# A gated mix of attention and feed-forward: the order of the first key and query products, of the last projection products, an eviction split in two, and the last stores

## The chip, the cores and the metric

The kernel runs on one NeuronCore of a Trainium2 chip. Its engines, as the profile names them, are PE (TensorE, matrix products, with PEld for its weight loads), DVE (VectorE), ACT (ScalarE), POOL (GpSimd) and SP (SyncE, which here issues most of the DMAs). The metric is device time in microseconds (us), lower is better. All times in this text are us unless marked otherwise; a time such as 12.80 is a place in the profiled execution, counted from the start of its span.

## The reference, cut to what matters

```python
x = A_x                                            # 1 x 2048 x 512, bf16
g = sigmoid((x * gate_w).sum(-1, keepdims=True))
q, k, v = split(x @ wqkv)                          # 32 heads of 16
p = softmax((q @ k.T) * 16 ** -0.5)
a = merge_heads(p @ v) @ wo
b = (silu(x @ w_gate) * (x @ w_up)) @ w_down       # 512 -> 1792 -> 512
return g * a + (1 - g) * b
```

## The kernel before, in words

The queries are cut into four blocks of 512 (`QB`), the heads into eight groups of four (`G`), which makes 32 units (`UNITS`) of 16 key tiles (`KT`). For each unit and key tile PE makes scores `s_t` in PSUM, two heads at a time in one tile of 128 x 1024; ACT turns each into `e_t` with one exponential; PE then multiplies it with the values into `o_ps`, the output product. A part of the tiles goes another way: PE makes `d_t`, and DVE computes the exponential of it in several steps over `y_t`, `z_t` and `u_t`, with an addition done by a DMA from POOL's queue. The first column of each head's values is one, so `o_ps` also holds the softmax denominators. When a unit is done, `post` (L900) evicts `o_ps` to `osb`.

Around this a planner in the kernel (`Plan`, `Pacer`) orders the other work, which is the projections of queries, keys and values and the feed-forward. It keeps estimated times of PE, DVE and ACT and writes each engine's instructions in one fixed order; `mm`, `act`, `vec` and `queue` record that order, so most instructions have the lines L158, L161 and L170 of these helpers. Each engine works through its own list in order. The planner starts its clocks after the opening, so the opening and the end are written out by hand.

**The opening (L178 to L1062).** The input is needed transposed, as `xT`: four blocks of 128 features (`dc` 0 to 3). For the first 1024 tokens, blocks 0 and 1 come by transposing DMAs, which SP issues one after the other; the rows of blocks 2 and 3 come by a plain DMA into `x_rows` (a part of `wd_t`) and are turned on PE by products with the identity (`turn`, L1022). Block 3's turned form is evicted by ACT into `xT`, block 2's by DVE in two halves. The weights of the first four heads come by ACT's queue and are spread by ACT into `wpad[1]` (keys) and `wpad[0]` (queries), with gaps between the heads; this is the padding copy of L241 to L244. `keep_warm` (L999) makes products whose result nobody reads. Then come the key products into `kp0` (two per block), the query products into `qp0` (one per block) and, after each block but the last, one `keep_warm`. Behind them:

- DVE takes the largest key of each row (`largest`, `kpart`) and makes a bound from it (`k_neg`, `kneg1`),
- ACT takes the size of the queries (`aq0`) and evicts the keys into `kaug`,
- PE makes the first values (`v0`, tile `vp`) and adds the bound to the queries (`bound_add`),
- DVE makes two variants of the queries from the sum (`q0a`); the first scores need them.

**The end (from L1451).** The last query block's output is `o @ wo`, scaled by the gate, for four tiles of 128 tokens (`tq` 0 to 3). All but the last unit's part is summed ahead: tiles 0 and 1 in `a_l_a` and `a_l_b`, tiles 2 and 3 in the two halves of one PSUM tile `al`, which takes a buffer of the scores. Each sum has five products (`last_rows`): three with normalised heads (`on`), one with the unit before the last (`osb`, `wo_l`), one that brings in the feed-forward part (`bblk`, `ident`). `tail(0)` writes the first five of al's ten products ahead of the last output product, `tail(1)` the other five behind it. For the last unit the denominators are gathered by four small products `dt`, inverted by DVE (`rt`), spread by sixteen small products `rps`, multiplied by DVE into `on_l` (four pieces), and four more products finish the sums. DVE scales and evicts tiles 0 and 2, ACT tiles 1 and 3, and each of the four tiles is stored by its own DMA of 128 KB, from SP for DVE's and from ACT's queue for ACT's.

Of the kernel before, what the change touches and what calls it, by code (L numbers as in the profile page):

```python
# [8 lines left out]
ACT = mybir.ActivationFunctionType  # L9
# [3 lines left out]
F32 = mybir.dt.float32  # L13
# [66 lines left out]
def kernel(  # L80
# [12 lines left out]
    nc = tc.nc  # L93
    P = 128
# [6 lines left out]
    NB = H // 8  # L101
    DC = D // P
    FC = F // P
    KT = S // P
    QBW = 512
    QB = S // QBW
    TQ = QBW // P
    assert H * DH == D and D % P == 0 and F % P == 0 and S % QBW == 0 and G == 8 and TQ == 4
    out_f = out.flatten_outer_dims()
    inv_sqrt_dh = 1.0 / math.sqrt(DH)  # L110
    VC = DH + 1
    UNITS = QB * G
# [26 lines left out]
    ps_s = ctx.enter_context(tc.tile_pool(name="ps_s", bufs=2, space=bass.MemoryType.PSUM))  # L139
# [6 lines left out]
    def ordered(ins):  # L146
        i = ins.ins
        if i.engine in last_of:
            tc.add_manual_dep(
                i, last_of[i.engine].name,  # L150
                mybir.DependencyInfo(mybir.DependencyClass.NoSync, mybir.DependencyReason.DATA),
                reason="order",
            )
        last_of[i.engine] = i
        return ins

    def mm(*args, **kw):
        return ordered(nc.tensor.matmul(*args, **kw))  # L158

    def act(*args, **kw):  # L160
        ordered(nc.scalar.activation(*args, **kw))  # L161
# [10 lines left out]
    vec = Ordered(nc.vector)  # L172
    queue = Ordered(nc.sync)
# [11 lines left out]
    for c0 in (D, 0):  # L185

        nc.scalar.dma_start(out=wqk[:, :, c0:c0 + 64],
                            in_=A_wqkv[:, c0:c0 + 64].rearrange("(dc p) c -> p dc c", p=P))
# [6 lines left out]
    for c0 in (D, 0):  # L195
        queue.dma_start(out=wqk[:, :, c0 + 64:c0 + D],
                          in_=A_wqkv[:, c0 + 64:c0 + D].rearrange("(dc p) c -> p dc c", p=P))
# [19 lines left out]
    mt = big.tile([P, FC, QBW], BF16, name="mt")  # L217
# [20 lines left out]
    def ones_rows(engine, g):  # L238

        engine.memset(kaug[:, g, :].bitcast(F32), 1.0019378662109375)  # L240
    for i in (1, 0):  # L241
        act(out=wpad[i][:, :, :].rearrange("p dc (j c) -> p dc j c", c=32)[:, :, :, 1:1 + DH],
            in_=wqk[:, :, i * D:i * D + 64].rearrange("p dc (j c) -> p dc j c", c=DH), func=ACT.Copy)
        ones_rows(nc.vector, 2 - i)  # L244
    ident = const.tile([P, P], BF16, name="ident")
    nc.gpsimd.memset(ident[:], 1.0)
    nc.gpsimd.affine_select(out=ident[:], in_=ident[:], pattern=[[-1, P]], compare_op=ALU.is_equal,
# [13 lines left out]
    for h in range(8):  # L261
        c = 2 * (h % 4) + h // 4
# [29 lines left out]
    owed = []  # L292
# [19 lines left out]
    def spend_v(cost, ready=0.0, key=None):  # L312

        if key is not None and key == plan.last:
            cost += 0.13
        plan.last = key
        plan.dve = max(plan.dve, ready) + cost

    def pay(i=0):
        ready, cost, f, c, key = owed.pop(i)  # L320
        spend_v(cost, ready, key)
        keep, plan.chain = plan.chain, None
        f()
        plan.chain = keep
        if c is not None:
            c.owed -= 1
            if c.done():
                c.done_at = plan.slot

    def m_ready(n=1):  # L330

        t = sorted(b for b in banks if b is not None)
        return t[n - 1] if len(t) >= n else None

    def stuck():
        if d_wait:
            pay_d()
        elif owed:
            pay()
        else:  # L340
            emit_piece(pace.cur)

    def m_tile(name):
        while m_ready() is None:
            stuck()
        i = min((i for i in range(3) if banks[i] is not None), key=lambda i: banks[i])
        plan.pe = max(plan.pe, banks[i])
        banks[i] = None
        held[i] = ps_m[i].tile([P, QBW], F32, tag=f"m{i}", name=name)
        return held[i]  # L350
# [15 lines left out]
    def force(c):  # L366
        for a in c.after + c.begun:
            force(a)
        while not c.out():
            while c.cond is not None and not c.cond():  # L370
                if owed:
                    pay()
                else:
                    for f in at.pop(min(at)):
                        f()
            emit_piece(c)
        while c.owed:
            pay()
# [292 lines left out]
    scaled = set()  # L671
# [180 lines left out]
    o_of = {}  # L852
    closed = 0
    o_end = [0.0]
    done_a = [0] * UNITS
    pvs = [0] * UNITS
# [33 lines left out]
    osbs = {}  # L890
# [9 lines left out]
    def post(un):  # L900
        qb, g = UNIT[un]
        osbs[un] = osb0[qb] if g == 0 else work.tile([P, QBW], BF16, tag="osb", name="osb")
        if un == 0:
            assert part_scaled
            vec.tensor_tensor(out=osbs[un][:, :], in0=o_of.pop(un)[:, :], in1=o_part, op=ALU.add)
        else:
            vec.tensor_copy(out=osbs[un][:, :], in_=o_of.pop(un)[:, :])

# [10 lines left out]
    def recip16(o, i):  # L919
        with nc.allow_low_precision(reason="bf16 reciprocal of softmax denominators is plenty accurate here"):  # L920
            vec.reciprocal(o, i)
# [36 lines left out]
    here_done = []  # L958
    a_ps = []
# [9 lines left out]
            a_ps.extend([pa, pb])  # L969
        return two_banks(NB + 1, "a_l", last_rows(0), last_rows(1), keep, stop=False)  # L970

    def tail(k):

        if k == 0:
            for c in sorted(pace.chains, key=lambda c: c.deadline):
                force(c)
            while owed:
                pay()
            assert here_done and len(scaled) == TQ
            al = ps_s.tile([P, 2 * QBW], F32, tag="s", name="al")  # L980
            a_ps.extend([al[:, 0:QBW], al[:, QBW:2 * QBW]])
        todo = [(tq, i) for tq in (2, 3) for i in range(NB + 1)]
        for tq, i in todo[:5] if k == 0 else todo[5:]:
            w, r = last_rows(tq)(i)
            mm(a_ps[tq][:, 0:D], lhsT=w, rhs=r, start=(i == 0), stop=False)

# [12 lines left out]
    def keep_warm(n):  # L999
        for _ in range(n):  # L1000
            mm(warm[:, :], lhsT=idle[:, 0:P], rhs=idle[:, :], start=True, stop=True)
# [26 lines left out]
    tp = ps_s.tile([P, 2 * QBW], F32, tag="s", name="tp")  # L1028
    turn(DC - 1, [tp[:, 0:QBW], tp[:, QBW:2 * QBW]])
    act(out=xT[:, DC - 1, 0:2 * QBW], in_=tp[:, :], func=ACT.Copy)  # L1030
    tps = [m_tile("tp") for _ in range(2)]
    turn(DC - 2, tps)
    for k in range(2):
        vec.tensor_copy(out=xT[:, DC - 2, k * QBW:(k + 1) * QBW], in_=tps[k][:, :])
        m_free(tps[k], 0.0)
    keep_warm(1)
    arrived = (0, 3, 2, 1)
    for dc in arrived:
        for tb in range(2):
            mm(kp0[:, tb * QBW:(tb + 1) * QBW], lhsT=wpad[1][:, dc, :], rhs=xT[:, dc, tb * QBW:(tb + 1) * QBW],  # L1040
               start=(dc == arrived[0]), stop=(dc == arrived[-1]))
        mm(qp0[:, :], lhsT=wpad[0][:, dc, :], rhs=xT[:, dc, 0:QBW], start=(dc == arrived[0]), stop=(dc == arrived[-1]))
        if dc != arrived[-1]:
            keep_warm(1)
    largest(0, kp0[:, :])
    k_neg(kneg1, 0, idle[:, 0:P])
    act(out=aq0, in_=qp0[:, :], func=ACT.Abs)
# [19 lines left out]
    pace = Pacer()  # L1067
# [60 lines left out]
    for qb in range(1, QB):  # L1128
        d = qb * KT
# [5 lines left out]
    for qb in range(QB):  # L1135
        for b in range(NB):
            d = UNIT.index((qb, max(2 * b, 1))) * KT
# [30 lines left out]
    for qb in range(QB):  # L1168
# [18 lines left out]
        for tq in range(TQ):  # L1187
            c = pace.add(down_pieces(qb, tq), 0 if qb else 100, a0 + per * (0.6 + 0.3 * (tq + 1) / TQ if qb < QB - 1 else 0.68 + 0.32 * (tq + 1) / TQ), (gus if tq == 0 else prev) + fin_prev + gates)
# [202 lines left out]
    while au < UNITS:  # L1391
# [10 lines left out]
        if room > 0.02:  # L1402
# [6 lines left out]
            c = side(room + SLACK)  # L1409
# [23 lines left out]
        n = au * KT + at_  # L1433
# [5 lines left out]
    while closed < UNITS or vops or added or vcur:  # L1439
        fill_dve()  # L1440
        while owed and owed[0][0] <= plan.pe:
            pay()
        if plan.slot < SLOTS + 1:
            begin(plan.slot + 1)
            pace.credit = max(pace.credit, 2.0)
        if vcur:
            emit_d()
            continue
        c = side(2.0)
        if not pv_list(plan.pe) and c is not None:  # L1450
            put_piece(c)  # L1451
            continue
        if closed == UNITS - 1 and pvs[closed] == KT - 1:
            tail(0)
        next_pv()
    for c in sorted(pace.chains, key=lambda c: c.deadline):
        force(c)
# [10 lines left out]
    assert not at  # L1468
    un = UNITS - 1
    osb = osbs[un]  # L1470
    tail(1)
    dt = m_tile("dt")
    for tq in range(TQ):
        mm(dt[:, 4 * tq:4 * tq + 4], lhsT=osb[:, tq * P:(tq + 1) * P], rhs=sel_t[:, :], start=True, stop=True)
    rt = work.tile([P, 4 * TQ], BF16, tag="rt", name="rt")
    recip16(rt[:, :], dt[:, 0:4 * TQ])
    rps = ps_s.tile([P, 2 * QBW], F32, tag="s", name="rps")
    for tq in range(TQ):
        for j in range(4):
            mm(rps[32 * j:32 * j + 32, tq * P:(tq + 1) * P],  # L1480
               lhsT=rt[:, 4 * tq + j:4 * tq + j + 1].broadcast_to([P, 32]), rhs=ident[:, :],
               start=True, stop=True, tile_position=(0, 32 * j), skip_group_check=True)
    on_l = work.tile([P, QBW], BF16, tag="rd", name="on_l")
    for tq in range(TQ):
        cs = slice(tq * P, (tq + 1) * P)
# [4 lines left out]
    for tq in range(TQ):  # L1490
        t = (QB - 1) * TQ + tq
        if tq % 2 == 0:
            vec.tensor_scalar(out=mt[:, tq, :], in0=a_ps[tq][:, 0:D], scalar1=gval[:, t:t + 1], scalar2=None, op0=ALU.mult)
        else:
            act(out=mt[:, tq, :], in_=a_ps[tq][:, 0:D], func=ACT.Identity, scale=gval[:, t:t + 1])
        (queue if tq % 2 == 0 else nc.scalar).dma_start(out=out_f[t * P:(t + 1) * P, :], in_=mt[:, tq, :])

# [28 lines left out]
```

## Time and profile before

| | us |
|---|---|
| median of 4 runs | 830.71 |
| the runs | 830.58, 832.01, 830.29, 830.85 |
| the profiled execution, its time | 832.21 |
| the profiled execution, its span from first to last instruction | 830.5 |
| busy in the span: PE, DVE, ACT, POOL | 787.1, 795.6, 810.9, 102.2 |
| first exponential starts | 14.56 |
| last exponential ends | 821.65 |
| mean granted PE clock | 0.996 |

The profiled execution is 1.50 longer than the median of the runs, and 0.20 longer than the longest of them. Of its time 1.71 lies outside the span. The busy times are sums over the whole span; the views by stretch tell where each engine is full. In a timeline line the columns are start, duration, engine, source line, operation, what is written from what with the shapes, how many, and in brackets the idle time before it and what ended it. A tile's name is followed by `<-` and its inputs, and buffer numbers are left out. Equal instructions that follow each other closely are merged into one line.

### The profile page before, as it was taken

What the parts mean: (1) busy time and instruction counts of PE and PEld (TensorE: products, weight loads), DVE (VectorE), ACT (ScalarE), POOL (GpSimd) and SP (SyncE); (2) the same over time, 40 slices, a digit from 0 to 9 for tenths busy, and PEclk for the clock granted to TensorE, in tenths of its full rate; (3) what the DMA queues carried; (4) which work ended last, traced back from release to release, by engine and by line L of the source; (5) the groups of instructions that cost most, each with busy time, mean ns of one, the idle gap of its engine ahead of it and who ended that gap; (6) DMA issues with size and microseconds to landing.
All of it is one profiled execution on the core that took longest, in us unless ns stands there. A gap on an engine that the chain in (4) does not pass through costs nothing. (4 is left out here: it accounts for less than half of the span.)

```text
span 830.5 us, 20397 instructions
## 1 busy us (share of the span) xinstructions
PE 787.1 (95%) x8118; PEld 233.7 (28%) x8119; DVE 795.6 (96%) x1175; ACT 810.9 (98%) x912; POOL 102.2 (12%) x124
## 2 busy tenths in 40 slices
PE   8999999999999999999999999999998999999996
PEld 3322332322222222222222222222222222222222
DVE  6799999999999999999999999999999999999994
ACT  4999999999999999999999999999999999999996
POOL 5010011010001100101111110101111101111100
PEclk9999999999999999999999999999999999999999
DMA  7034346565544445564444464544435365453323
GB/s 178 2 64 89 71 88 130 120 146 102 111 102 84 81 90 124 107 125 82 82 82 95 84 141 86 122 91 97 80 64 111 78 123 112 102 100 71 77 61 77
DMA packets 100647, 79.54 MB, mean 96 GB/s; under 512 B 75696, under 2 KB 88584, under 8 KB 100552
## 3 DMA queue, kind: packets, MB, share of 16 engines
q0 software_dynamic: 12960, 47.19, 30.7%
q1 hardware_dynamic: 85720, 30.60, 15.9%
q8 instruction: 63, 1.03, 0.5%
q10 hardware_dynamic: 1872, 0.46, 0.3%
q14 instruction: 32, 0.26, 0.1%
HBM read 21.36 MB, written 2.34 MB: 29 GB/s over the span
## 5 line engine op out<-in xcount | busy, mean ns | idle before, releaser
L161 ACT ACTIVATE e_t<-s_t 128x1024 bf16<-128x1024 f32 x844 | 787.8, 1110 | 3.6 <-PE s_t L158 3.4
L158 PE MATMUL s_t<-qx,kaug 64*128 64x512 bf16 x1336 | 274.0, 383 | 24.9 <-ACT e_t L161 21.5
L170 DVE TENSOR_SCALAR y_t<-d_t 128x512 uint16<-128x512 f32 x360 | 234.4, 681 | 1.4 <-PE d_t L158 1.2
L158 PEld LDWEIGHTS <-kaug 64*128 64x128 bf16 x2048 | 111.8, 93 | 340.6 <-issue 331.1
L158 PE MATMUL o_ps<-e_t,vaug 128*32 128x512 bf16 x1688 | 168.1, 390 | 0.3 <-DVE osb L170 0.3
L158 PE MATMUL d_t<-qx,kaug 64*128 64x512 bf16 x296 | 102.0, 380 | 2.3 <-DVE y_t L170 1.5
L792 POOL DMA_DIRECT2D y_t<-u_t x45 | 44.4, 988 | 362.0 <-PE s_t L158 178.5
L158 PEld LDWEIGHTS <-vaug 128*32 128x32 bf16 (+1 forms) x2060 | 50.7, 93 | 122.8 <-issue 121.8
L158 PE MATMUL gu<-xT,wg 128*32 128x512 bf16 x896 | 76.8, 383 | 0.1
L158 PE MATMUL dps<-wd_t,mt 128*32 128x512 bf16 x896 | 76.1, 383 | 0.2
L792 POOL DMA_DIRECT2D y_t<-kaug x39 | 40.5, 1038 | 283.7 <-DVE kaug L170 108.1
L158 PE MATMUL gu<-xT,wu 128*32 128x512 bf16 x896 | 73.4, 382 | 0.1
L170 DVE TENSOR_SCALAR y_t<-y_t 128x2048 uint16<-128x2048 uint16 x90 | 61.5, 684 | 6.5 <-DMA y_t<-u_t 3.8
L170 DVE TENSOR_SCALAR z_t<-y_t 128x2048 uint16<-128x2048 uint16 x90 | 61.8, 687 | 1.0
L170 DVE TENSOR_TENSOR u_t<-u_t 128x2048 f16<-128x2048 f16 x45 | 55.0, 1221 | 0.9
L170 DVE TENSOR_TENSOR u_t<-u_t,z_t 128x2048 f16<-128x2048 f16 x45 | 54.7, 1215 | 0.1
L170 DVE TENSOR_TENSOR kaug<-kaug 128x2048 f16<-128x2048 f16 x39 | 47.7, 1222 | 0.9
L158 PE MATMUL s_t<-q,kaug 64*128 64x512 bf16 x212 | 43.5, 383 | 4.7 <-ACT e_t L161 4.2
L170 DVE TENSOR_TENSOR kaug<-kaug,z_t 128x2048 f16<-128x2048 f16 x39 | 47.4, 1216 | 0.1
L170 DVE SCALAR_TENSOR_TENSOR mt<-gs,gu 128x512 bf16<-128x512 bf16 x56 | 38.2, 683 | 2.4
L161 ACT ACTIVATE th<-gu 128x512 bf16<-128x512 f32 x56 | 38.2, 682 | 0.0
L170 DVE SCALAR_TENSOR_TENSOR gs<-th,gu 128x512 bf16<-128x512 bf16 x56 | 37.9, 677 | 0.1
(134 smaller groups left out, 560.1 us busy)
## 6 DMA issues: line engine op xcount, KB each, us to landing
y_t<-u_t POOLq DMA_DIRECT2D x45, 512.0 KB, 5.0
y_t<-kaug POOLq DMA_DIRECT2D x39, 512.0 KB, 5.1
wg<-in_B_w_gate_dram SPq DMA_DIRECT2D x56, 128.0 KB
wu<-in_B_w_up_dram SPq DMA_DIRECT2D x56, 128.0 KB
y_t<-wd_t POOLq DMA_DIRECT2D x6, 512.0 KB, 5.0
on<-osb SPq DMA_DIRECT2D x120, 16.0 KB
rb<-rr SPq DMA_DIRECT2D x15, 128.0 KB
wd_t<-in_B_w_down_dram SPq DMA_DIRECT2D x7, 256.0 KB
```

What stands on the lines that cost most here:

```text
L158: return ordered(nc.tensor.matmul(*args, **kw))
L161: ordered(nc.scalar.activation(*args, **kw))
L170: return lambda *a, **kw: ordered(f(*a, **kw))
L792: nc.gpsimd.dma_start(out=ya, in_=ua, accum_op=ALU.add)
```

## The change

There are five edits, the first two in the opening and the other three at the end:

1. The padding copy of the query weights (`pad(0)`) stands behind ACT's eviction of the turned block, no longer ahead of it.
2. All eight key products stand ahead of the four query products; the blocks are taken in the order 0, 2, 3, 1 and not 0, 3, 2, 1; the three `keep_warm` products between the blocks are gone.
3. The ten products of `al` are taken by kind and not by tile, and spread in other places: three ahead of the last two output products, three behind them, two behind `dt`, two behind `rps`.
4. The last `osb` is evicted in two halves of 256 columns, one by DVE and one by ACT.
5. The four stores of 128 KB become two of 256 KB, tiles 0 and 1 from SP and tiles 2 and 3 from ACT's queue.

```diff
-    for i in (1, 0):
+    def pad(i):
         act(out=wpad[i][:, :, :].rearrange("p dc (j c) -> p dc j c", c=32)[:, :, :, 1:1 + DH],
             in_=wqk[:, :, i * D:i * D + 64].rearrange("p dc (j c) -> p dc j c", c=DH), func=ACT.Copy)
-        ones_rows(nc.vector, 2 - i)
+
+    pad(1)
+    for g in (1, 2):
+        ones_rows(nc.vector, g)
...
+        elif un == UNITS - 1:
+            o = o_of.pop(un)
+            vec.tensor_copy(out=osbs[un][:, 0:QBW // 2], in_=o[:, 0:QBW // 2])
+            act(out=osbs[un][:, QBW // 2:QBW], in_=o[:, QBW // 2:QBW], func=ACT.Copy)
         else:
             vec.tensor_copy(out=osbs[un][:, :], in_=o_of.pop(un)[:, :])
...
-    def tail(k):
-
-        if k == 0:
-            for c in sorted(pace.chains, key=lambda c: c.deadline):
-                force(c)
-            while owed:
-                pay()
-            assert here_done and len(scaled) == TQ
-            al = ps_s.tile([P, 2 * QBW], F32, tag="s", name="al")
-            a_ps.extend([al[:, 0:QBW], al[:, QBW:2 * QBW]])
-        todo = [(tq, i) for tq in (2, 3) for i in range(NB + 1)]
-        for tq, i in todo[:5] if k == 0 else todo[5:]:
+    rest = [(tq, i) for i in range(NB + 1) for tq in (2, 3)]
+
+    def tail_ready():
+        for c in sorted(pace.chains, key=lambda c: c.deadline):
+            force(c)
+        while owed:
+            pay()
+        assert here_done and len(scaled) == TQ
+        al = ps_s.tile([P, 2 * QBW], F32, tag="s", name="al")
+        a_ps.extend([al[:, 0:QBW], al[:, QBW:2 * QBW]])
+
+    def tail(n):
+
+        for _ in range(n):
+            tq, i = rest.pop(0)
             w, r = last_rows(tq)(i)
             mm(a_ps[tq][:, 0:D], lhsT=w, rhs=r, start=(i == 0), stop=False)
...
     act(out=xT[:, DC - 1, 0:2 * QBW], in_=tp[:, :], func=ACT.Copy)
+    pad(0)
     tps = [m_tile("tp") for _ in range(2)]
...
-    arrived = (0, 3, 2, 1)
+    arrived = (0, 2, 3, 1)
     for dc in arrived:
         for tb in range(2):
             mm(kp0[:, tb * QBW:(tb + 1) * QBW], lhsT=wpad[1][:, dc, :], rhs=xT[:, dc, tb * QBW:(tb + 1) * QBW],
                start=(dc == arrived[0]), stop=(dc == arrived[-1]))
+    for dc in arrived:
         mm(qp0[:, :], lhsT=wpad[0][:, dc, :], rhs=xT[:, dc, 0:QBW], start=(dc == arrived[0]), stop=(dc == arrived[-1]))
-        if dc != arrived[-1]:
-            keep_warm(1)
...
-        if closed == UNITS - 1 and pvs[closed] == KT - 1:
-            tail(0)
+        if closed == UNITS - 1 and pvs[closed] >= KT - 2 and not a_ps[2:]:
+            tail_ready()
+            tail(3)
         next_pv()
...
-    tail(1)
+    tail(3)
     dt = m_tile("dt")
...
     recip16(rt[:, :], dt[:, 0:4 * TQ])
+    tail(2)
     rps = ps_s.tile([P, 2 * QBW], F32, tag="s", name="rps")
...
+    tail(len(rest))
     on_l = work.tile([P, QBW], BF16, tag="rd", name="on_l")
...
-        (queue if tq % 2 == 0 else nc.scalar).dma_start(out=out_f[t * P:(t + 1) * P, :], in_=mt[:, tq, :])
+        if tq % 2:
+            (queue if tq == 1 else nc.scalar).dma_start(
+                out=out_f[(t - 1) * P:(t + 1) * P, :].rearrange("(i p) d -> p i d", p=P), in_=mt[:, tq - 1:tq + 1, :])
```

In the instruction lists that the two kernels build, everything between the opening and the last output products stands in the same order on every engine.

## The prediction

> **What bounds the kernel now.** I read the busy times of stretches first, because the edits touch only the first 15 us and the last 12. Columns: stretch, its length, busy us of PE, PEld, DVE, ACT, POOL, granted PE clock, DMA share, GB/s.
>
> ```profile
> 26.00:800.00 774.00, 742.47 (x7710) 217.94 (x7709) 761.86 (x1107) 772.61 (x869) 89.22 (x88) 1.00 0.48 96
> ```
>
> ACT is busy 772.61 of 774.00 us, with exponentials. So a head start of the exponentials is handed on to the last one, and a saving behind the last one counts in full. Next the timeline of the start (start us, us, engine, line, operation, what ended the idle time):
>
> ```profile
> 7.40 0.44 ACT L161 ACTIVATE mt<-wqk 128x256 bf16<-128x256 bf16 x1 [1.28 <-DMA wqk<-in_A_wqkv_dram]
> 7.73 1.00 ACT L161 ACTIVATE xT<-tp 128x1024 bf16<-128x1024 f32 x1
> ...
> 11.13 1.23 DVE L170 TENSOR_REDUCE kpart<-kp 128x1 f32<-128x1024 f32 x1 [3.11 <-PE kp L158]
> ...
> 12.80 0.40 PE L158 MATMUL qp<-mt 128*32 128x512 bf16 x4 [0.56 <-DVE mt L170]
> 13.33 1.41 DVE L170 TENSOR_SCALAR mt<-qp,vsel 128x512 bf16<-128x512 f32 x2 [0.58 <-PE qp L158]
> ...
> 14.56 1.03 ACT L161 ACTIVATE e_t<-s_t 128x1024 bf16<-128x1024 f32 x1 [0.57 <-PE s_t L158]
> ```
>
> The first exponential stands at the end of one chain: key products, their maximum, the bound, the query variants, the scores. The eviction of the turned block sat behind a padding copy that waited for a DMA until 7.40. The clock comes from windows of 3.41 us:
>
> ```profile
> 5.30:8.71 3.41, 2.86 (x24) 1.49 (x23) 1.29 (x2) 1.76 (x3) 3.02 (x13) 1.00 1.32 224
> ...
> 12.13:15.54 3.41, 1.65 (x20) 0.61 (x20) 2.63 (x6) 2.58 (x4) 0.00 (x0) 1.00 1.02 287
> 15.54:18.95 3.41, 3.41 (x28) 0.69 (x20) 3.18 (x7) 1.99 (x3) 0.00 (x0) 0.50 0.46 158
> ```
>
> In the window from 12.13 PE was busy 48%, and in the next its clock is 0.50: five key pieces (20 products) take 15.12 to 17.0, where five at the usual 0.216 would need 1.1. The chain of waits gives the end:
>
> ```profile
> 820.91 0.34 PE o_ps L158 x4
> 821.25 0.32 PE al L158
> 821.57 0.05 issue
> 821.62 0.81 PE al L158 x3
> 822.44 0.33 PE o_ps L158 x4
> 822.77 1.19 PE al L158 x5
> 823.95 0.09 PE dt L158 x4
> 824.04 0.02 issue
> 824.07 0.27 DVE rt L170
> 824.34 0.04 issue
> 824.38 0.44 PE rps L158 x16
> ```
>
> The last exponential ended at 821.65, but its output product waited for five projection products, to 822.37; then five more kept dt from an osb that was ready at 823.51.
>
> **What the skill says.** "TensorE: Matmul & The Clock Gate", Part 1: PE's clock halves after an idle window of about 3.4 us, and the windows run free of the kernel. The trace agrees in size (15.54 to 18.95 is 3.41), and shows that 48% busy is idle enough while 84% (first window) is not. "PSUM — Partial Sum Buffer", PSUM bank collisions: ACT and DVE may not read one bank's quadrant at once, even in different columns; they have to be ordered. The trace agrees for one tile: ACT's read of al at 827.07 waited 0.56 for DVE's. "DMA: Bandwidth & Descriptors", Anatomy of one DMA: most of a DMA's fixed time lies behind its last byte. Here the last store's packets end near 829.15 and the span at 830.5.
>
> **Start.** Removed: three warming products (0.216 each). Moved: four query products behind eight key products, the second padding copy behind the turned block's eviction, and block 2 ahead of block 3. No DMA moves.
> 1. Turned block: its products end near 6.4, so ACT evicts from about 6.5 to 7.5, off the path; the padding copy then runs to about 7.95, and the query products need it only after 9.
> 2. Key products: the first still waits for its transposed block until 7.69. Six products at 0.216 end at 8.98. The seventh needs the other transposed block, of which before shows only that it was there by 10.50. In the DMA view SP's queue had moved 2064 packets by 6.2 and 3204 by 8.0; the rows of x and each transposed block take 1040. So the first block's packets ended near 6.4 (seen at 7.69) and the second's, at 3120, near 7.9; with a like delay it lands near 9.15. So the last key product starts at 9.37, not 10.72: the maximum starts at about 9.80 instead of 11.13, **1.33 earlier**. Bounds: 1.5 with no wait, 0 if the block lands near 10.4.
> 3. Bound: maximum 1.23 and k_neg 0.35 allow it at 11.45. PE first does four query products (0.86) and vp (1.10) from 9.58, to 11.5. So 11.5, not 12.80.
> 4. Query variants, scores and exponential keep their distances (12.80 to 14.56 is 1.76): first exponential 13.28, **1.28 earlier**. ACT's key eviction moves from 12.39 to 11.25 behind Abs and ends at 12.37, before the scores at 12.86. DVE's and PE's later work hangs on the same products and moves along. The later loads are in time: the last block of xT has its packets by 12.6, so lands near 13.8, and the fourth of the key pieces needs it near 14.5; the rest of the weights, by 17.3, has later users.
>
> The clock is a second effect. With pieces at 0.216 the third exponential of before would start at 16.7, not 17.67, and the fourth at 17.6, not 19.15: the slow window cost this execution about **1.5**. It took 832.21 us; the runs' median is 830.71, with 830.29, 830.58, 830.85 and one at 832.01. The gap of 1.50 is what the slow window costs, so I take it that most timed runs don't have it: it needs a window that holds the idle stretch. After the change PE idles about 1.2 us in that stretch (11.9 to 12.86, 13.25 to 13.52) instead of 1.8, so a window is at least 64% busy, which should spare the clock. Against the median this gives nothing.
>
> **End.**
> 1. Two of the five projection products go behind the last output product. PE: three al from 820.85, two output products from 821.61 and 821.83 (the exponential ends at 821.65). The last ends near 822.23 instead of 822.77: **-0.54**.
> 2. osb is split: 256 columns on DVE, 256 on ACT. By the instructions of the changed program as built, ACT waits for DVE's half, not for PE. DVE: 448 columns took 0.619 and 512 0.682, so 256 about 0.42. ACT copies: 512 took 0.59, 1024 0.996, so 256 about 0.39. In series, with the 0.03 seen at al: 0.84 instead of 0.69, **+0.15**; osb is whole at 823.12. ACT's waits on old DMAs are long over. Bounds: -0.3 if the halves overlapped, +0.3 with a slower hand-over.
> 3. dt's second half needs ACT's half: recip at 823.47 instead of 824.07. Of the other seven al products three lie under the eviction, two under recip, two under on_l. The last two hold the first on_l product to about 824.82 (825.18 before), so DVE's a_l_a eviction starts at 825.26, not 825.64, and the last ACT eviction at 826.69, not 827.07: **-0.38** is left.
> 4. Two stores of 256 KB for four of 128. The last now starts 0.38 earlier but carries twice the bytes. Before, its packets took 0.52 us for 128 KB, at up to 358 GB/s; another 128 KB is **+0.36**. Issue: 0.36 before; other DMAs with 512 and 1024 rows took 0.46 to 0.74, so 0 to +0.3 more. On SP the first store now waits for ACT's half too (825.96), with no store behind it; its packets are gone before the last one's.
> Sum of the end: about 0, from -0.3 to +0.5.
>
> **Forecast:** -1.28 and about 0: -1.3 on 830.71, **829.4 us**. A measurement of this kernel can tell about 0.2%, 1.66 us, from no change, so this counts as no difference, though it should be a real gain.
>
> **Rivals.**
> A, the forecast, 60%: 828.7 to 830.0 of its own (start 1.1 to 1.5, end -0.3 to +0.4, median's noise); about a third of it lies beyond 1.66, most of that because before's own runs hold a slow window now and then.
> B, the slow window is in all of before's runs and gone after, and the profile's 1.5 us are its overhead: -1.3 -1.5 = **827.9**. For it: the window stands plainly in the trace. Against: three of four runs lie 1.4 below the other. 22%.
> C, the transposed block lands near 10.4: the key products wait, and the query products are pushed behind them: gain at most 0.2, **830.5**. Only the bound of 10.50 speaks for it; the packet count against. 13%.
> D, slower: without the warming products and with PE waiting for blocks, a window from about 7 to 10.4 counts as idle, and query products, vp, bound, scores and key pieces run at half clock: +0.9, +0.7, +0.2, +0.2 and +1.1 is 3.1, less 1.3: **832.5**. It decides if the limit lies above the 80% that PE would be busy there; 84% held the clock. 5%, of which 3 are slower by over 1.66.
>
> **Chances.** Faster: 20 from A and 22 from B, 0.42. Slower: 0.03. Same: the rest of A, C and D, 0.55. Range: 827.7 to 830.3 holds A, most of B and part of C.
>
> **What would show it.** First exponential near 13.3, maximum near 9.8, seventh key product waiting for a DMA until about 9.15; no 0.50 stretch after 15. At the end, last output product 0.2 after the last exponential's end instead of 0.7; ACT's osb half starting just as DVE's ends; a last store whose packets take about 0.9. I'd be wrong in the start if the key products waited past 9.6, in the end if the last store's packets took as long as before.

## The result, and the profile after

| | before | after |
|---|---|---|
| median of the runs | 831.02 (53 runs, 830.16 to 833.08) | 829.52 (34 runs, 828.29 to 832.59) |
| the profiled execution, its time | 832.21 | 829.32 |
| its span | 830.5 | 827.6 |
| first exponential starts | 14.56 | 13.33 |
| last exponential ends | 821.65 | 818.85 |

The ratio is 0.998, with a 95% interval of 0.9975 to 0.9985: a gain of 1.50 us, just inside the 0.2% that were called no difference. One run of e1 (1581.61) and one of the runs of before beside e1 to e4 (3272.12) lie far outside all the others and are left out of every interval and count below.

The busy times of the middle stretch, in the columns of before:

```profile
26.00:797.00 771.00, 739.63 (x7687) 216.97 (x7683) 758.99 (x1101) 769.90 (x866) 89.19 (x88) 1.00 0.48 96
```

ACT is busy 769.90 of 771.00, so it still bounds the kernel; how much of a head start it hands on is read further down. The timeline of the opening of after:

```profile
6.97 1.02 ACT L161 ACTIVATE xT<-tp 128x1024 bf16<-128x1024 f32 x1 [0.82 <-PE tp L158]
...
7.89 0.43 ACT L161 ACTIVATE mt<-wqk 128x256 bf16<-128x256 bf16 x1
7.94 1.89 PE L158 MATMUL kp<-xT,mt 128*128 128x512 bf16 x8 [0.35 <-DMA xT<-in_A_x_dram]
...
9.87 1.22 DVE L170 TENSOR_REDUCE kpart<-kp 128x1 f32<-128x1024 f32 x1 [1.38 <-PE kp L158]
...
11.56 0.40 PE L158 MATMUL qp<-mt 128*32 128x512 bf16 x4
...
13.33 1.94 ACT L161 ACTIVATE e_t<-s_t 128x1024 bf16<-128x1024 f32 x2 [0.51 <-PE s_t L158]
...
15.51 2.86 ACT L161 ACTIVATE e_t<-s_t 128x1024 bf16<-128x1024 f32 x3 [0.24 <-PE s_t L158]
```

The eight key products are one line of 1.89, so nothing stops them once they have begun; the maximum follows at 9.87, the bound at 11.56 with no idle bracket in front of it, the first exponential at 13.33 and the third at 15.51. The same stretches of 3.41 us as before show that the clock stays up:

```profile
12.12:15.53 3.41, 2.36 (x30) 0.94 (x34) 3.08 (x5) 2.66 (x5) 0.00 (x0) 1.00 1.03 282
15.53:18.94 3.41, 3.41 (x44) 0.85 (x36) 3.34 (x8) 3.41 (x4) 0.00 (x0) 1.00 0.48 167
```

The granted clock (third column from the end) is 1.00 in both, where before had 0.50 in the second. ACT is full there (3.41) where it had 1.99. The chain of waits at the end of after:

```profile
818.87 0.57 PE o_ps L158 x8
819.45 0.02 issue
819.47 0.44 DVE osb L170
819.91 0.02 issue
819.93 0.39 ACT osb L161
820.32 0.05 issue
820.37 0.20 PE dt L158 x2
820.57 0.45 PE al L158 x2
821.02 0.36 PE rps L158 x16
821.39 0.02 issue
821.41 0.88 DVE on_l L170 x4
822.29 0.66 DVE mt L170
822.96 0.67 DVEq L1538
823.63 0.02 issue
823.65 0.69 ACT mt L161
```

The last output product no longer stands behind five projection products; the two halves of `osb` stand one behind the other; and the last eviction, ACT's, stands behind DVE's (822.96 to 823.65).

**Where the time came from, in the profiled pair.** I followed the start of the n-th exponential in both traces. Before is later by 1.23 at the first, by 2.72 at the fourth, by 2.79 at the last (820.47 against 817.68). From the last exponential's end the span goes on for 8.75 after and 8.85 before, 0.10 less. So 832.21 - 829.32 = 2.89 is 1.23 (the chain of the opening) + 1.49 (the slow clock window, which before's profiled run had) + 0.07 (the middle) + 0.10 (the end).

A caution goes with this sum. The builds e3, e4, e7, e10 and e12 below have their first exponential within 0.06 of after's, and up to the 140th each keeps its distance from after to 0.02; but their last one starts between 0.89 earlier (e10) and 1.45 later (e4). So one pair of traces shows only to about a microsecond how much of a head start reaches the end.

**In the medians.** Of before's 53 runs, 18 are above 831.5; the median of the other 35 is 830.72. After has one run in 34 above 831.5; but its runs lie lower, so the same limit catches fewer of them: three (830.58, 830.66 and 832.59) lie 1.0 or more above its median. So 1.20 of the 1.50 is there against the lower runs of before too, and 0.30 comes from the share of the higher ones; what the 1.20 is made of the medians don't say (see e5). Over all the sets of runs of before below, 59 of 149 are above 831.5, the medians of the two parts lying 1.5 to 1.6 apart in each set, which is close to the 1.49 that the slow window cost in the profiled run.

### The profile page after: what moved, and what is told of

It reads as the page before. It is cut to its first block, busy times and chain, and to the rows that moved or that the text cites. A ratio compares the mean times of both kernels' runs of the same rounds, so it can differ in the third digit from the quotient of the medians.

```text
span 827.6 us, 20391 instructions
## 1 busy us (share of the span) xinstructions
PE 785.2 (95%) x8115; PEld 233.0 (28%) x8116; DVE 795.0 (96%) x1175; ACT 811.2 (98%) x913; POOL 102.2 (12%) x124
```

## The experiments

Theory: the gain is the head start of the opening's chain, about 1.25, and the end gives nothing. Rivals: the gain is the slow clock window alone; the end gains and loses something that cancels. "Stretch" is the time from the start of the last exponential to the end of the span, which the traces give to a hundredth (830.51 before, 827.61 after): 10.04 before, 9.93 after. The medians of before beside the runs were 830.91 (e1 to e4), 831.41 (e5 to e8) and 831.40 (e9 to e12).

**e1 and e8: the edits of the opening alone.** The kernel before, with

```diff
-    for i in (1, 0):
+    def pad(i):
...
+    pad(0)
...
-    arrived = (0, 3, 2, 1)
+    arrived = (0, 2, 3, 1)
...
+    for dc in arrived:
...
-        if dc != arrived[-1]:
-            keep_warm(1)
```

> The kernel before with the two edits of the opening alone (padding copy behind the eviction; key products ahead of query products, no warming products between). If the gain comes from the opening and is handed on to the last exponential: first exponential near 13.3 (14.56 before), the stretch from the last exponential's end to the span's end unchanged at 8.85, median 1.2 to 1.7 below before. If the gain comes from the end: first exponential earlier, but the last one ends where it did, median within 0.3 of before.

Measured: 829.92 (829.0 to 831.06 without the profiled run), ratio 0.9979, interval 0.9971 to 0.9986. That is 0.99 below before, where 1.2 to 1.7 was expected. The profile belongs to the run of 1581.61, so e8 is the same kernel with another profile.

> Once more the opening's edits alone, for a profile. First exponential near 13.3, no 0.50 window before 20 us, fourth exponential near 16.4; from the last exponential's start to the span's end 10.0, as before (10.03), against 9.9 in the changed kernel.

Measured: 830.97. First exponential at 13.30, no slow window in the opening, stretch 10.09 where 10.0 was expected. But there is one in the middle of the kernel; two windows of e8:

```profile
459.11:462.52 3.41, 2.29 (x20) 0.93 (x16) 3.27 (x6) 3.00 (x4) 0.12 (x1) 1.00 0.88 140
462.52:465.93 3.41, 3.41 (x21) 0.49 (x20) 2.81 (x4) 2.33 (x3) 1.36 (x1) 0.50 0.45 96
```

In the first PE is busy 2.29 of 3.41, 67%; in the second the clock is 0.50, and ACT's 2.33 of 3.41 shows it starved. The exponentials were 0.12 ahead of after's before it and 1.63 behind after it. So one slow window costs 1.75 here, far from the opening. What set it off isn't shown: in e3 a window at the same place (459.13 to 462.55) is as empty (2.31 of 3.42), and the clock behind it stays at 1.00. As to the gain, e1's interval covers that of the whole change (0.9975 to 0.9985), so within what these runs can tell the opening's edits bring all of it.

**e2: the edits of the end alone.** The kernel before, with

```diff
-            tail(0)
+            tail_ready()
+            tail(3)
...
+            vec.tensor_copy(out=osbs[un][:, 0:QBW // 2], in_=o[:, 0:QBW // 2])
+            act(out=osbs[un][:, QBW // 2:QBW], in_=o[:, QBW // 2:QBW], func=ACT.Copy)
...
-    tail(1)
+    tail(3)
...
+        if tq % 2:
```

> The kernel before with the three edits of the end alone (order of the al products, osb split, two stores). If the opening carries the gain: first exponential near 14.56, last exponential's end to the span's end 8.7 to 8.8 instead of 8.85, median within 0.3 of before. If the end carries it: that stretch 7.5 or less, median 1.3 or more below before.

Measured: 831.73, ratio 1.0004, interval 0.9996 to 1.0012; stretch 9.95. The end gives nothing that can be measured. Eight of its 13 runs are above 831.5, and its profile has the slow window of before; two windows of e2:

```profile
11.53:14.94 3.41, 1.65 (x34) 1.02 (x30) 2.79 (x5) 2.40 (x4) 0.46 (x1) 1.00 1.11 254
14.94:18.35 3.41, 3.41 (x28) 0.87 (x30) 3.02 (x7) 1.73 (x3) 0.00 (x0) 0.50 0.64 219
```

It begins at 14.94, where before's began at 15.54 with the same first exponential (14.61 and 14.56): the window doesn't follow the kernel.

**e3: four stores again.** The kernel after, with

```diff
-        if tq % 2:
-            (queue if tq == 1 else nc.scalar).dma_start(
-                out=out_f[(t - 1) * P:(t + 1) * P, :].rearrange("(i p) d -> p i d", p=P), in_=mt[:, tq - 1:tq + 1, :])
+        (queue if tq % 2 == 0 else nc.scalar).dma_start(out=out_f[t * P:(t + 1) * P, :], in_=mt[:, tq, :])
```

> The changed kernel with the four stores of 128 KB as before. If the time of the last store goes with its bytes: its packets take 0.5 instead of 0.9, the stretch from the last exponential's end to the span's end is 8.35 instead of 8.75, median 0.4 below the changed kernel. If what counts is a fixed time per store: the stretch stays within 0.1 of 8.75.

Measured: 829.13, ratio 0.9977, interval 0.9969 to 0.9985; stretch 9.41 instead of 9.93. The last store is issued 6.69 after the last exponential's start in both, so the 0.52 comes behind that: the last packet ends 1.39 after the issue instead of 1.81, which is 0.42 of transfer, and the span ends 1.33 behind it instead of 1.43. What the DMA engines moved from 820 to 830, in slices of 0.25 us, in after:

```profile
GB/s 0 0 0 0 0 0 0 0 0 0 0 0 0 0 0 0 262 352 356 78 0 262 352 348 86 0 0 0 0 0 0 0 0 0 0 0 0 0 0 0
```

and in e3:

```profile
GB/s 0 0 0 0 0 0 0 0 0 0 0 0 0 0 0 0 0 315 328 340 340 250 147 340 37 0 0 0 0 0 0 0 0 0 0 0 0 0 0 0
```

After has two heaps of four slices with a gap; the first one is over before the second begins, so the second, 256 KB, is paid in full. In e3 three stores are moved before the packets of the last one begin, and the last heap is half as long.

**e4: `osb` evicted whole.** The kernel after, with

```diff
-        elif un == UNITS - 1:
-            o = o_of.pop(un)
-            vec.tensor_copy(out=osbs[un][:, 0:QBW // 2], in_=o[:, 0:QBW // 2])
-            act(out=osbs[un][:, QBW // 2:QBW], in_=o[:, QBW // 2:QBW], func=ACT.Copy)
```

> The changed kernel with the last osb evicted whole by DVE. If the two halves run one after the other and so cost: osb whole 0.69 after the last output product instead of 0.84, the reciprocal about 0.1 earlier, the stretch from the last exponential's end to the span's end about 8.65 instead of 8.75. If the split helps because two of the four dt products then run ahead: the reciprocal 0.1 later, the stretch 8.85.

Measured: 829.49, ratio 0.998, interval 0.9972 to 0.9988; stretch 9.83 instead of 9.93. The timeline of e4:

```profile
820.92 0.69 DVE L170 CAST osb<-o_ps 128x512 bf16<-128x512 f32 x1 [1.41 <-PE o_ps L158]
821.67 0.25 PE L158 MATMUL dt<-sel_t,osb 128*128 128x4 bf16 x4
...
821.96 0.26 DVE L170 RECIPROCAL rt<-dt 128x16 bf16<-128x16 f32 x1 [0.35 <-PE dt L158]
```

and of after:

```profile
819.47 0.42 DVE L170 CAST osb<-o_ps 128x256 bf16<-128x256 f32 x1 [1.62 <-PE o_ps L158]
819.93 0.38 ACT L161 ACTIVATE osb<-o_ps 128x256 bf16<-128x256 f32 x1 [1.07 <-DVE osb L170]
...
820.61 0.26 DVE L170 RECIPROCAL rt<-dt 128x16 bf16<-128x16 f32 x1 [0.71 <-PE dt L158]
```

From the eviction's start to the reciprocals' it is 1.04 whole and 1.14 split: the two halves run in turn, as predicted, and the split costs 0.10, which is also what the stretch shows.

**e5: only the idle stretch filled.** The kernel before, nothing moved, with six products that nobody reads:

```diff
     v0(0)
+    keep_warm(2)
     bound_add(qp0, kneg1, aq0)
+    keep_warm(4)
```

> The kernel before with six more warming products in PE's idle stretch of the opening: two ahead of bound_add, four behind it; nothing else is moved. If a third of before's runs are 1.5 us longer because PE is idle enough there for a slow clock window: no 0.50 window before 20 us, first exponential at 14.6 as before, fourth near 17.6, runs above 831.5 at most 1 in 10 (18 of 53 before), median 0.3 to 0.6 below before. If the longer runs have another cause: their share stays about a third, median within 0.15 of before.

Measured: 829.78 (829.51 to 830.48, ten runs), ratio 0.9977, interval 0.9968 to 0.9987: as much as the whole change, though its first exponential stands at 14.61. I moved a window of 3.41 along the opening of each trace and took the place where PE is busy least. Before:

```profile
11.41:14.82 3.41, 1.65 (x37) 1.02 (x33) 2.79 (x5) 2.40 (x4) 0.58 (x1) 1.00 1.00 246
```

after:

```profile
10.20:13.61 3.41, 2.20 (x43) 1.41 (x40) 2.76 (x5) 2.37 (x4) 1.78 (x3) 1.00 0.99 183
```

e5:

```profile
11.48:14.89 3.41, 2.96 (x41) 1.34 (x38) 2.79 (x5) 2.40 (x4) 0.52 (x1) 1.00 1.01 221
```

That is 48%, 65% and 87%. None of e5's runs is above 831.5, where 15 of 34 runs of before beside it are. So the slow window of the opening does come from idle PE time, and filling that time takes it away. This explains 0.46 of e5's 1.63 (the 19 lower runs of before beside it have a median of 830.95). The other 1.17 I had not expected, and the first exponential can't hold it. e7 below, which has after's opening, makes it plainer, since it ran beside e5: its first exponential is 1.27 earlier than e5's, but its last one only 0.30, and its median is 829.74 against 829.78. Between these two the head start is not found in the runs, and so the 1.20 of the change isn't shown to be the head start either.

In the profiles, e5's exponentials lag after's by 1.28 until the 142nd and by 0.71 at the last; the largest steps are at the 143rd (0.30) and the 658th (0.16). Near these two places and the 472nd there are steps of 0.1 to 1.0, either way, in most of the other traces, the largest in e4 at the 658th: there ACT waits 0.15 to 0.9 for a score product, or doesn't. In after, ACT's waits in the whole middle come to

```profile
ACT e_t L161 <- PE s_t L158: 1.0, 5, 0.3
```

(1.0 us in five waits, the longest 0.3); before has 1.6. What decides at these places isn't settled, and with one trace of each build neither is whether it belongs to the build or to the run.

**e6: the query products between the key products again,** without warming. The kernel after, with

```diff
-    for dc in arrived:
         mm(qp0[:, :], lhsT=wpad[0][:, dc, :], rhs=xT[:, dc, 0:QBW], start=(dc == arrived[0]), stop=(dc == arrived[-1]))
```

(the line then falls into the key products' loop).

> The changed kernel with the query products again after each block's two key products, still without warming products. If the order counts: the last key product comes three products later (0.65), the maximum near 10.5, the first exponential near 13.95 instead of 13.3, and half of the opening's gain is gone. If leaving out the warming products were the whole gain: first exponential at 13.3.

Measured: 830.76 (829.67 to 832.99), ratio 0.9994, interval 0.9986 to 1.0001. The timeline of e6:

```profile
10.57 1.23 DVE L170 TENSOR_REDUCE kpart<-kp 128x1 f32<-128x1024 f32 x1 [2.37 <-PE kp L158]
...
14.01 1.94 ACT L161 ACTIVATE e_t<-s_t 128x1024 bf16<-128x1024 f32 x2 [0.58 <-PE s_t L158]
```

The maximum is 0.70 later than in after (three query products of 0.216 are 0.65), the first exponential 0.68. So of the 1.23 won at the first exponential, 0.68 is the order of the products, and 0.55 is left for the other edits of the opening, of which the three warming products (3 x 0.216 is 0.65) are large enough to be all. Its idlest window:

```profile
10.84:14.25 3.41, 1.64 (x36) 1.02 (x33) 2.78 (x5) 2.39 (x4) 1.14 (x2) 1.00 1.04 216
```

It is as empty as before's (48%), and 7 of its 20 runs are above 831.5. The profiled run isn't one of them, and its trace shows why: the clock's own windows lie elsewhere. In every trace here that has changes of the clock, the time between two of them is a whole number of steps of 3.413 (in e8 it is 457.39, which is 134 of them). In e6 the first change is at 5.73, so the windows counted on from there are 9.14 to 12.56, 84% busy, and 12.56 to 15.97, 64% busy, and the clock stays at 1.00. The 13 lower runs have a median of 830.22, 0.48 above e7's 829.74 beside it, with first exponentials 0.67 apart; so here the head start does reach the runs, for the most part. With the query products in front, PE waits for the maximum; behind the key products they fill that wait. The move thus does two things at once, and here both can be seen: without it the chain is later, and the runs above 831.5 are back.

**e7: the padding copy ahead again.** The kernel after, with

```diff
     pad(1)
+    pad(0)
...
-    pad(0)
```

> The changed kernel with the padding copy of the query weights again ahead of the turned block's eviction. If that eviction has room: it ends near 8.7, the third block's key products wait at most 0.25, first exponential 13.3 to 13.6. If the copy was what held the key products: first exponential near 14.3.

Measured: 829.74 (829.11 to 830.72), ratio 0.9976, interval 0.9966 to 0.9986. The timeline of e7:

```profile
7.75 1.00 ACT L161 ACTIVATE xT<-tp 128x1024 bf16<-128x1024 f32 x1
7.96 1.89 PE L158 MATMUL kp<-xT,mt 128*128 128x512 bf16 x8 [0.84 <-DMA xT<-in_A_x_dram]
...
13.34 1.94 ACT L161 ACTIVATE e_t<-s_t 128x1024 bf16<-128x1024 f32 x2 [0.50 <-PE s_t L158]
```

The turned block is evicted 0.78 later, to 8.75, and the first exponential moves by 0.01: the fifth key product, the first to need it, starts at 8.82 anyway. Edit 1 is worth nothing here; 0.07 more and it would have been worth something.

**e9: the last tile in a PSUM tile of its own.** Both evictions of `al` read one tile. The kernel after, with

```diff
-        al = ps_s.tile([P, 2 * QBW], F32, tag="s", name="al")
-        a_ps.extend([al[:, 0:QBW], al[:, QBW:2 * QBW]])
+        a_ps.extend([ps_s.tile([P, 2 * QBW], F32, tag="s", name="al")[:, 0:QBW], m_tile("al3")])
...
-    dt = m_tile("dt")
+    rps2 = ps_s.tile([P, 2 * QBW], F32, tag="s", name="rps")
+    dt, rps = rps2[:, 0:QBW], rps2[:, QBW:2 * QBW]
...
-    rps = ps_s.tile([P, 2 * QBW], F32, tag="s", name="rps")
```

> The changed kernel, with the last projection tile's accumulator in a PSUM tile of its own (the denominators' products move to the tile of the reciprocals' instead), so that ScalarE's last eviction of the kernel need not wait for VectorE's eviction of the neighbouring half, which it did for 0.56 us. If that wait is a real one on the path that sets the end: the last eviction about 0.5 earlier, stretch from the last exponential's start to the end of the span 9.4 instead of 9.92, median 0.5 under the changed kernel's. If the last store is paced by the first one's packets or by its own landing: the eviction moves and the end does not, 9.9.

Measured: 829.34, ratio 0.9975, interval 0.9964 to 0.9987; stretch 9.46, 0.47 less. The timeline of e9:

```profile
822.70 0.74 DVE L170 TENSOR_SCALAR mt<-al,gval 128x512 bf16<-128x512 f32 x1
822.81 0.68 ACT L161 ACTIVATE mt<-al,gval 128x512 bf16<-128x512 f32 x1
```

The two evictions overlap now, and ACT's has no idle bracket; it starts 0.66 earlier, counted from the last exponential's start (5.31 instead of 5.97). Of that, 0.19 is lost again behind it: the first store is issued as late as before (5.44 after that start, 5.43 in after), and the last one's packets now follow on its packets without a gap.

**e10: three stores as well.** The kernel of e9, with tiles 0 and 1 in one store, tile 2 in one from SP, tile 3 in one from ACT's queue:

```diff
-        if tq % 2:
-            (queue if tq == 1 else nc.scalar).dma_start(
+        if tq:
+            (queue if tq < 3 else nc.scalar).dma_start(
...
```

> The kernel of e9, with three stores: tiles 0 and 1 together, tile 2 and tile 3 alone, so that the last one is 128 KB again. If the two gains at the end add up (0.5 for the tile of its own, 0.47 measured for four stores): stretch 9.0, median 0.9 to 1.0 under the changed kernel's, ratio 0.9965 or so. If the last store's landing is a fixed time whatever its size: 9.4.

Measured: 828.66 (827.77 to 829.29), ratio 0.9963, interval 0.995 to 0.9976; but the stretch is 9.46, the same as e9's, where 9.0 was expected if the gains added up. What the DMA engines moved from 820 to 830 in e10:

```profile
GB/s 0 0 0 0 0 0 0 0 0 0 0 0 119 332 356 344 348 328 267 4 0 0 0 0 0 0 0 0 0 0 0 0 0 0 0 0 0 0 0 0
```

One heap without a gap: 0.52 MB at 328 to 356 GB/s, some 1.6 us, begun by the first store. Now the transfers are full from the first store to the last, and the last one's size decides nothing. The 0.68 of the median's gain over e9 must then lie in front of the end: in the profiles e10's exponentials are 0.16 later than e9's at the 130th and 0.71 earlier at the last, mostly by steps near the 143rd and the 472nd. That part isn't the end's doing.

**e11: the idle stretch filled in the kernel after,** with `keep_warm(4)` behind `bound_add`.

> The changed kernel with four warming products behind the bound's addition in the opening. If the few slower runs of the changed kernel come from a slow clock window in the opening that idle TensorE time brings on: the same first exponential (13.33, within 0.1), the same fast runs, and no run over 1 us above the fastest cluster. If slow windows elsewhere make them: the same share of slower runs, about one in ten. Median 829.3 to 829.6 on either.

Measured: 829.25 (828.81 to 829.6, eight runs), ratio 0.997, interval 0.996 to 0.998. The idlest window is 92% busy now, and no run stands apart; but with three in after's 34 that lie 1.0 or more above its median, eight runs can't tell. The first exponential of its profile is at 13.66, not within the 0.1 expected. The timeline of e11 shows why:

```profile
7.58 1.29 DVE L170 CAST xT<-tp 128x512 bf16<-128x512 f32 x2 [2.39 <-PE tp L158]
...
8.01 2.15 PE L158 MATMUL kp<-xT,mt 128*128 128x512 bf16 x8
```

The turned block 2 is whole at 8.87 (7.58 + 1.29), and the fourth key product, which needs its second half, starts at 8.92 instead of 8.65; the eight take 2.15 instead of 1.89. That is ahead of the added products. So the order 0, 2, 3, 1 puts a block early whose eviction by DVE is in time by 0.11 in after (7.19 + 1.29 is 8.48, needed at 8.59), and not in time in every run.

**e12: all together,** e10 with e11's four products and with `osb` whole as in e4.

> The kernel of e10 with the four warming products of e11 and the last output block evicted whole by VectorE. Split and whole were equal to 0.1 us before, so: as e10 within 0.1 at the end (stretch 9.0 to 9.1), median within 0.3 of e10's. If the split was worth something that the wait for the last tile covered: 0.15 longer than e10.

Measured: 828.65 (827.87 to 830.24), ratio 0.9967, interval 0.9955 to 0.9979; stretch 9.38, against 9.46 of e10. So the split costs 0.08 here, about what it cost in e4. e10 and e12 are the fastest versions, 0.6 under e11 beside them; they are also 0.9 under the median of after, which was measured beside another set of before (831.02).

## Why the prediction was right

829.4 was forecast and 829.52 measured. The opening went by rival A's course almost to the hundredth; that the median is met to 0.12 is in part luck, as the first and the fourth point show. Step by step:

- **The head start is handed on: right in the profiled pair, not shown in general.** It is 1.23 at the first exponential and, leaving out the slow window, 1.30 at the last. Up to the 140th exponential it held in every trace that was compared. Behind that, a busy ACT (769.90 of 771.00) still left steps of up to 1.0; e7 against e5 has 0.30 left of 1.27, and e5 gained 1.17 over before's lower runs with no head start at all. The forecast had no term for either.
- **Key products, maximum, bound, first exponential: right.** 9.80, 11.5 and 13.28 were forecast; 9.87, 11.56 and 13.33 came. All are late by the same 0.05 to 0.07.
- **The seventh key product's wait: wrong in both terms, which cancelled.** It was to wait for a transposed block until near 9.15, so that the last began at 9.37. It waited for nothing; in e9 it started at 9.06, so the block was there by then. But the first began at 7.94 and not at 7.69, since its own block landed 0.25 later in that run, and seven steps of 0.216 from 7.94 are 9.45. Rival C, a landing near 10.4, is excluded.
- **The slow window, 1.5 and mostly absent from the timed runs: right in size, too low in share.** The profiled pair shows 1.49. "Most timed runs don't have it" holds, but four in ten do, and that is worth 0.30 of the median's gain, for which the forecast put nothing. It stays within the range, and rival B, which put its 1.5 into all runs, doesn't fit the two groups of before's runs, with medians of 830.72 and 832.31. An estimate of the share from before's trace alone: a window of 3.41 is no more than 49% busy if it starts between 11.38 and 12.25, which is a quarter of the places where it can start.
- **"At least 64% busy, which should spare the clock": the outcome was right, the ground too weak.** The idlest place of after is 65% busy. The page "TensorE: Matmul & The Clock Gate" of the Trainium skill, Part 1, says that the clock halves after an idle window; how idle it has to be, the traces here show in part. What counts is the clock's own window and not any stretch of that length (e6). Of those windows in the openings, the two of 48% (before, e2) were followed by half clock, and those of 64% (e6), 66% (e3, e8, e9) and 68% (e7) were not. But one of 67% was, in the middle of e8, so 65% is no proof against it.
- **The end, step 1: right.** The last output product starts 0.18 after the last exponential's end; 0.2 was forecast.
- **Step 2: right.** DVE 0.42, hand-over 0.04, ACT 0.38: 0.84 in series, as worked out, and e4 shows the price against the whole eviction, 0.10 for the 0.15 forecast. One reading behind this step doesn't hold: ACT's wait of 0.56 on `al` was taken as agreeing with the rule on one bank. Each half of `al` is written by products of 512 columns of its own, and the wait is an order that the program as built has for two reads of one tile, so it is no evidence for that rule. No run here lets two engines read one bank at once.
- **Step 3: mis-sized.** The reciprocals are 0.66 earlier, counted from the last exponential's end (-0.60 forecast), but the last eviction is 0.62 earlier and not 0.38. The term that failed is the hold of two `al` products on the first `on_l` product "to about 824.82", 3.17 after the exponential's end. It starts 2.91 after it, 0.35 after `on_l`'s start, as before (0.34): the two products fit in front of it.
- **Step 4: mis-sized the other way.** The bigger last store was put at 0.36 and measured 0.52 (e3), inside its bounds. So the end is -0.62 + 0.52 = -0.10 where about 0 was forecast; e2 shows that no median can tell.

Rival D, slower through a slow clock among the key products, didn't come: the eight take 1.89 in after, at 0.216 from one to the next.

## What to carry to other kernels

Take the head of a chain that ends in the engine that bounds the kernel, and put on the other engines only what the chain needs; the work moved behind is then best placed where its engine would have waited anyway, because there it also keeps PE's clock up. Then look whether the head start reaches the end: behind the 140th exponential this kernel won or lost up to a microsecond of it in steps. A stretch of a few us in which PE is half idle was worth filling here with products that nobody reads, and whether a kernel has this trouble is read from two groups of run times, not from one profile. At the end of a kernel, count each saving down to the last transfer: it was here handed from eviction to store size to the DMA engines' throughput, and each step was hidden until the one before was taken away.

## What the runs showed of the hardware

- The windows of the clock run free: the slow one began at 14.94 in one run and at 15.54 in another with openings 0.05 apart, and it came once at 462.52, in the full middle of the kernel. A stretch that is 48% busy slowed the clock where it filled such a window (before, e2) and not where two windows shared it (e6).
- Two evictions of one PSUM tile by DVE and ACT ran in turn in these builds, by the program's order (0.56 of waiting); in two tiles they overlapped, with unchanged durations (0.74 and 0.68).
- At the end of the kernel, 0.52 MB of stores took some 1.6 us at up to 356 GB/s, if they followed without a gap (e10), and the span ended 1.33 after the last packet with four stores (before, e3) and 1.43 to 1.45 after it with two or three (after, e9, e10, e12), whether the last had 128 or 256 KB.
- The middle of the kernel differed by up to 2.3 us between single traces of builds whose instructions there stand in the same order (e10 against e4). The large steps were near the same few exponentials, the 142nd, the 472nd and the 658th; the cause stays open.
